# Reordering the layer-norm prologue and splitting the last output tiles of a linear-attention block

## The chip, the core and the metric

The kernel runs on one core of a Trainium2 chip. The metric is the device time of one execution in microseconds (us). The span in a profile is 1.4 to 1.8 us shorter than this time, and the difference will matter below. All times inside a profile count from the start of its span. PE is the matrix engine (PEld its weight loads), DVE is VectorE, ACT ScalarE, POOL GpSimd, SP SyncE.

## The reference

Layer norm of x, then a linear-attention branch s (32 heads of 20) and a gate g from a two-layer ReLU block, with S = 2048, D = 640, Dff = 1728, all bf16:

```python
xn = _layernorm(x, axis=-1)
s = _A_ref(xn, A_wqkv, A_wo)        # phi(q), phi(k): linear attention, then @ wo
g = _silu(_B_ref(xn, B_w1, B_w2))   # relu(xn @ w1) @ w2
return x + s * g
```

## The kernel before

The program is a list of operations per engine. Each engine runs its own list in order, and a helper derives the semaphore waits from what each operation reads (`R`) and writes (`W`). The 2048 tokens are 16 tiles of 128. Two places are touched: the head, in which tiles 0 to 3 are loaded, normalised and transposed and their keys computed, and the tail, in which the last two tiles are multiplied by g, added to x and stored.

```python
    KS = 3                                   # wk is loaded as 3 + 2 row blocks
    x_load(0)
    x_load(1)
    w_load(wqk[:, 0:KS, D:2 * D], A_wqkv[0:P * KS, D:2 * D], ("wk", 0))
    x_load(2)
    w_load(wqk[:, KS:C, D:2 * D], A_wqkv[P * KS:D, D:2 * D], ("wk", 1))
    x_load(3)
    # ... (cut)
    warm(34)                                 # matmuls without use, to wake PE's clock
    # ... (cut)
    # LN_stat(t, a): sums of half a of tile t (DVE).  LN_aggr: mean, variance (DVE).
    # LN_root_pool: 1/sqrt(var + eps) (POOL).  LN_stats = both LN_stat, LN_aggr, LN_root_pool.
    # LN_norm: (x - mean) * rs (DVE).  transposes: 5 on PE.  xnT_copy: PSUM to SBUF (ACT).
    # K_mm(t, bank, ks): 2 matmuls of 320 columns for each row block k in ks.
    LN_norm(0, late_loads)
    transposes(0, 4)
    warm(11)
    xnT_copy(0, 4)
    LN_stat(1, 1)
    LN_aggr(1)
    LN_root_pool(1)
    LN_stats(2)
    LN_norm(1)
    K_mm(0, 0, range(0, KS))
    transposes(1, 5)
    xnT_copy(1, 5)
    K_mm(0, 0, range(KS, C))
    LN_norm(2)
    warm(3)
    transposes(2, 6)
    xnT_copy(2, 6)
    K_mm(1, 2)
    K_exp(0, 0)
    K_relu(0, 0)
    LN_stats(3)
    LN_norm(3)
    K_mm(2, 5, range(0, KS))
    transposes(3, 4)
    xnT_copy(3, 4)
    K_mm(2, 5, range(KS, C))
    warm(3)
    # ... (cut: keys of tile 3, then queries, hidden layer, G, kv, W; U = second layer of the gate)
    U(0, kv_all)
    U(1, w_all)
    for p in range(2, 8):                    # U runs its hook between its two halves
        ts = pairs[p - 2] if p < 7 else pairs[5] + pairs[6]
        U(p, s_hook(ts, 0 if p % 2 == 0 else 4))
    pr[0] = 2
    for t in pairs[7]:
        s_tile(t, last=True)                 # last: multiply, add and store by halves
```

## Time and profile before

| | |
|---|---|
| time, median of 3 (at prediction) | 226.27 us (226.17 to 226.44) |
| span of the profiled run | 224.6 us |
| PE busy | 97% of the span |
| first weight load of the query matmuls | 14.17 us |
| end of PE's last matmul | 221.04 us |
| end of the last add on VectorE | 222.29 us |

Lines of the page of the kernel before: span, busy time by engine, PE's busy tenths and the granted clock in 40 slices, and the chain that ended last by engine.

```profile
span 224.6 us, 3494 instructions
...
PE 218.1 (97%) x1450; PEld 135.2 (60%) x1460; DVE 102.5 (46%) x191; ACT 88.3 (39%) x146; POOL 43.8 (20%) x62
...
PE   7999999999999999999999999999999999999993
...
PEclk9999999999999999999999999999999999999999
...
PE 92%; DVE 2%; DMA 2%; issue 1%; ACT 1%; SPq 1%; POOL 0%; DVEq 0%
```

PE is less than 90% busy only in the first and in the last slice. A change that leaves the real matmuls alone can gain time only there.

The head, from the chain of waits of the kernel before (start, us, what):

```profile
2.20 4.26 DMA reg<-in_A_x_dram
...
6.48 0.90 DVE stats L383 x2
7.40 0.22 DVE mv L387
...
7.70 0.32 POOL rsv L391
...
8.09 0.59 POOL rsy L393
...
8.70 0.46 DVE reg L412
...
9.21 0.45 PE psT L422 x5
9.66 2.17 PE psT L439 x16
11.83 0.32 PE psT L422 x5
...
12.17 0.71 ACT reg L427
...
12.93 1.55 PE psT L439 x10
```

The head hangs on the landing of x tile 2 at 6.48 us. Its sums, root and norm (8.70) lead to its transposes (9.21). Then come 16 key matmuls, the transposes of tile 3, their copy, and tile 3's matmuls at 12.93; the query matmuls follow without a gap.

The tail, from the timeline (start, us, engine, line, operation, shapes, count):

```profile
218.16 2.88 PE L796 MATMUL psT<-reg,pqT 128*128 128x320 bf16 x20
218.36 0.70 ACT L764 ACTIVATE reg<-psT 128x640 bf16<-128x640 f32 x1 [8.26 <-PE psT L768]
219.16 0.49 DVE L810 TENSOR_TENSOR reg<-psT,reg 128x320 bf16<-128x320 f32 x1 [2.99 <-ACT reg L764]
219.69 0.33 DVE L813 TENSOR_TENSOR reg<-reg 128x320 bf16<-128x320 bf16 x1
...
221.45 0.48 DVE L810 TENSOR_TENSOR reg<-psT,reg 128x320 bf16<-128x320 f32 x1
221.97 0.32 DVE L813 TENSOR_TENSOR reg<-reg 128x320 bf16<-128x320 bf16 x1
```

The last 20 matmuls end at 221.04. VectorE waits for the last silu (L764, ScalarE) and then works off four multiplies and four adds; the last ends 1.26 us past PE's end.

### The profile page before, as it was taken

What the parts mean: (1) busy time and instruction counts of PE and PEld (TensorE: products, weight loads), DVE (VectorE), ACT (ScalarE), POOL (GpSimd) and SP (SyncE); (2) the same over time, 40 slices, a digit from 0 to 9 for tenths busy, and PEclk for the clock granted to TensorE, in tenths of its full rate; (3) what the DMA queues carried; (4) which work ended last, traced back from release to release, by engine and by line L of the source; (5) the groups of instructions that cost most, each with busy time, mean ns of one, the idle gap of its engine ahead of it and who ended that gap; (6) DMA issues with size and microseconds to landing.
All of it is one profiled execution on the core that took longest, in us unless ns stands there. A gap on an engine that the chain in (4) does not pass through costs nothing.

```text
span 224.6 us, 3494 instructions
## 1 busy us (share of the span) xinstructions
PE 218.1 (97%) x1450; PEld 135.2 (60%) x1460; DVE 102.5 (46%) x191; ACT 88.3 (39%) x146; POOL 43.8 (20%) x62
## 2 busy tenths in 40 slices
PE   7999999999999999999999999999999999999993
PEld 7654555455554555444477778667767767776772
DVE  4599931796639872967000044440404041331445
ACT  4587765657665666654521122241021102102110
POOL 2436842322541255700000013000000000000000
PEclk9999999999999999999999999999999999999999
DMA  6999620012501150000999999500001010101021
GB/s 185 362 395 257 149 74 0 0 31 58 32 1 29 29 56 5 0 0 3 210 217 300 346 386 325 176 0 3 34 25 61 0 60 3 58 0 61 27 90 58
DMA packets 24239, 23.07 MB, mean 103 GB/s; under 512 B 8992, under 2 KB 23584, under 8 KB 24224
## 3 DMA queue, kind: packets, MB, share of 16 engines
q1 hardware_dynamic: 24224, 22.86, 35.7%
q8 instruction: 11, 0.18, 0.4%
q14 instruction: 4, 0.03, 0.1%
HBM read 15.65 MB, written 5.24 MB: 93 GB/s over the span
## 4 chain that ended last, share of the span: by engine, by line
PE 92%; DVE 2%; DMA 2%; issue 1%; ACT 1%; SPq 1%; POOL 0%; DVEq 0%
PE psT L768 25%; PE psT L514 25%; PE psT L702 10%; PE psT L491 10%; PE psT L439 9%; PE psT L796 8%; DMA reg<-in_A_x_dram 2%; PE psT L729 2%; PE psT L746 1%; PE psT L527 1%; DVE reg L810 1%; PE psT L714 1%; PE psT L610 1%; DVE reg L813 0%; DVE stats L383 0%
## 5 line engine op out<-in xcount | busy, mean ns | idle before, releaser
L768 PE MATMUL psT<-reg,hT 128*128 128x320 bf16 x416 | 58.7, 299 | 0.3
L514 PE MATMUL psT<-reg 128*128 128x512 bf16 x252 | 56.8, 379 | 0.5 <-issue 0.2
L768 PEld LDWEIGHTS psT<-reg,hT 128*128 128x128 bf16 x416 | 40.3, 98 | 17.0 <-PE psT L746 1.6
L514 PEld LDWEIGHTS psT<-reg 128*128 128x128 bf16 x260 | 25.2, 98 | 29.2 <-ACT hT L518 0.4
L764 ACT ACTIVATE reg<-psT 128x640 bf16<-128x640 f32 x16 | 10.8, 702 | 68.8 <-PE psT L746 35.4
L518 ACT ACTIVATE hT<-psT 128x512 bf16<-128x512 f32 x52 | 30.9, 599 | 17.7 <-PE psT L514 17.4
L810 DVE TENSOR_TENSOR reg<-psT,reg 128x640 bf16<-128x640 f32 (+1 forms) x18 | 13.5, 749 | 49.0 <-PE psT L796 45.9
L451 POOL TENSOR_TENSOR zacc<-zacc,reg 128x640 f32<-128x640 f32 x16 | 22.6, 1412 | 21.5 <-DVE reg L470 21.3
L439 PE MATMUL psT<-reg 128*128 128x320 bf16 x160 | 24.5, 299 | 0.1
L796 PE MATMUL psT<-reg,pqT 128*128 128x320 bf16 x160 | 22.9, 299 | 0.0
L702 PE MATMUL psT<-reg 128*128 128x320 bf16 x160 | 21.9, 299 | 0.0
L491 PE MATMUL psT<-reg 128*128 128x512 bf16 x98 | 21.8, 379 | 0.1
L439 PEld LDWEIGHTS psT<-reg 128*128 128x128 bf16 x160 | 15.4, 98 | 8.0 <-ACT reg L427 0.3
L702 PEld LDWEIGHTS psT<-reg 128*128 128x128 bf16 x160 | 15.6, 98 | 6.4 <-issue 0.4
L796 PEld LDWEIGHTS psT<-reg,pqT 128*128 128x128 bf16 x160 | 15.7, 98 | 6.1
L695 DVE TENSOR_TENSOR pqT<-pqT,reg 128x2048 bf16<-128x2048 bf16 x5 | 5.9, 1219 | 26.8 <-DMA reg<-rden_by_feature 26.8
L491 PEld LDWEIGHTS psT<-reg 128*128 128x128 bf16 x100 | 9.8, 98 | 11.2
L383 DVE BATCH_NORM_STATS2 stats<-reg 128x6 f32<-128x320 bf16 x32 | 14.1, 479 | 3.7 <-DMA reg<-in_A_x_dram 3.7
L498 ACT ACTIVATE er<-psT 128x512 bf16<-128x512 f32 x20 | 12.4, 619 | 8.6 <-PE psT L491 3.5
L456 ACT ACTIVATE ek<-psT 128x640 bf16<-128x640 f32 x16 | 11.3, 707 | 9.1 <-PE psT L439 9.1
L468 DVE TENSOR_SCALAR ek<-ek 128x640 bf16<-128x640 bf16 x16 | 5.5, 347 | 18.3 <-ACT ek L456 18.3
L508 DVE SCALAR_TENSOR_TENSOR pqT<-er 128x512 bf16<-128x512 bf16 x15 | 12.9, 859 | 0.5
(58 smaller groups left out, 139.2 us busy)
## 6 DMA issues: line engine op xcount, KB each, us to landing
reg<-in_A_x_dram SPq DMA_DIRECT2D x16, 160.0 KB, 5.3
rden_by_feature<-rden SPq DMA_DIRECT2D x4, 640.0 KB, 8.8
reg<-rden_by_feature SPq DMA_DIRECT2D x5, 512.0 KB, 11.1
reg<-in_A_x_dram SPq DMA_DIRECT2D x4, 640.0 KB, 6.8
reg<-in_B_w_dram SPq DMA_DIRECT2D x2, 1120.0 KB, 10.2
out_dram<-reg SPq DMA_DIRECT2D x14, 160.0 KB, 1.8
reg<-in_B_w_dram SPq DMA_DIRECT2D x1, 1040.0 KB, 10.2
reg<-in_B_w_dram SPq DMA_DIRECT2D x1, 960.0 KB, 14.8
```

Of the source, the lines that this page charges most:

```text
L383: sc.op("DVE", lambda eng: eng.bn_stats(stats[:, t, a, :], xin[:, t % XR, HN * a:HN * (a + 1)]), R=[("xin", t % XR)], W=[("stats", t, a)])
L439: fns.append(lambda eng, a=a, k=k: eng.matmul(ps[b + a][:, 0:HN], lhsT=xnT[:, k, tok(t)], rhs=wqk[:, k, D + HN * a:D + HN * (a + 1)], star ...
L451: sc.op("POOL", lambda eng: eng.tensor_tensor(out=zacc[:, :], in0=zacc[:, :], in1=pk[:, t, :], op=ALU.add), R=[("zacc",), ("pk", t)], W=[( ...
L491: sc.group("PE", [(lambda eng, k=k: eng.matmul(ps[b], lhsT=wqk[:, k, P * f:P * (f + 1)], rhs=xnT[:, k, schunk(j)], start=(k == 0), stop=(k ...
L498: sc.op("ACT", lambda eng: eng.activation(out=e_, in_=ps[b], func=ACTF.Exp), R=[("ps", b)], W=[("er_e", es)])
L508: sc.op("DVE", lambda eng: eng.scalar_tensor_tensor(out=pqT[:, f, schunk(j)], in0=e_, scalar=1.0, in1=r_, op0=ALU.min, op1=ALU.add), R=[(" ...
L514: a = sc.group("PE", [(lambda eng, k=k: eng.matmul(ps[b], lhsT=w1_sb[:, k, P * f:P * (f + 1)], rhs=xnT[:, k, schunk(j)], start=(k == 0), s ...
L518: sc.op("ACT", lambda eng: eng.activation(out=hT[:, f, schunk(j)], in_=ps[b], func=ACTF.Relu), R=[("ps", b)], W=[("hT", j, f)])
L702: fns.append(lambda eng, t=t, a=a: eng.matmul(ps[b + a][:, 0:HN], lhsT=xn[:, t, P * k:P * (k + 1)], rhs=pk[:, t, HN * a:HN * (a + 1)], sta ...
L768: fns = [(lambda eng, u=u, t=t, f=f, n=n: eng.matmul(ps[bs[n] + u][:, 0:HN], lhsT=hT[:, f, tok(t)], rhs=w2_sb[:, f, HN * n:HN * (n + 1)], ...
L796: sc.group("PE", [(lambda eng, c=c, a=a: eng.matmul(ps[b + a][:, 0:HN], lhsT=pqT[:, c, tok(t)], rhs=wf[:, c, HN * a:HN * (a + 1)], start=( ...
L810: sc.op("DVE", lambda eng: eng.tensor_tensor(out=tmpo[:, os_, lo:hi].rearrange(shp, a=na), in0=src, in1=g_sb[:, t, lo:hi].rearrange(shp, a ...
```

## The change

In the head, norm 1 is to run as soon as its root is there, between the two half sums of tile 2; tile 3 is loaded ahead of the rest of wk and its sums run ahead of norm 2; PE gets eight matmuls of tile 1 before the transposes of tile 2. In the tail, the left halves of the last two tiles move ahead of the last half of U; of the two right halves, one is added on GpSimd and stored from ScalarE's queue. The diff, cut to its core:

```diff
     x_load(2)
+    x_load(3)
     w_load(wqk[:, KS:C, D:2 * D], A_wqkv[P * KS:D, D:2 * D], ("wk", 1))
-    x_load(3)
-    warm(34)
+    warm(33)
# ... (cut)
-    LN_stats(2)
+    LN_stat(2, 0)
     LN_norm(1)
     K_mm(0, 0, range(0, KS))
     transposes(1, 5)
     xnT_copy(1, 5)
+    LN_stat(2, 1)
+    LN_aggr(2)
+    LN_root_pool(2)
+    warm(2)
     K_mm(0, 0, range(KS, C))
-    LN_norm(2)
-    warm(3)
-    transposes(2, 6)
-    xnT_copy(2, 6)
-    K_mm(1, 2)
     K_exp(0, 0)
     K_relu(0, 0)
     LN_stats(3)
+    LN_norm(2)
+    K_mm(1, 2, range(0, 4))
+    transposes(2, 6)
+    xnT_copy(2, 6)
+    K_mm(1, 2, range(4, C))
     LN_norm(3)
-    K_mm(2, 5, range(0, KS))
+    warm(3)
     transposes(3, 4)
     xnT_copy(3, 4)
-    K_mm(2, 5, range(KS, C))
-    warm(3)
+    K_mm(2, 5)
# ... (cut: s_half(t, a, bank, slot, addE, dmaE): 5 matmuls, multiply, add and store of half a of tile t)
-    for p in range(2, 8):
-        ts = pairs[p - 2] if p < 7 else pairs[5] + pairs[6]
-        U(p, s_hook(ts, 0 if p % 2 == 0 else 4))
-    pr[0] = 2
-    for t in pairs[7]:
-        s_tile(t, last=True)
+    for p in range(2, 7):
+        U(p, s_hook(pairs[p - 2], 0 if p % 2 == 0 else 4))
+    ea, eb = pairs[7]
+    oe = [(so[0] + 4) % NOUT, (so[0] + 5) % NOUT]
+    def last_hook():
+        s_hook(pairs[5] + pairs[6], 4)()
+        s_half(ea, 0, 0, oe[0])
+        s_half(eb, 0, 1, oe[1])
+    U(7, last_hook)
+    s_half(ea, 1, 4, oe[0], "POOL", "ACT")
+    s_half(eb, 1, 5, oe[1])
```

More of the change, by code (lines that the diff above doesn't have):

```diff
@@ L441, in K_mm @@
                     start=(k == 0), stop=(k == C - 1)))
-        wks = [0, 1] if ks is None else [0 if ks[0] < KS else 1]
+        wks = [0, 1] if ks is None else sorted({0 if k < KS else 1 for k in ks})
         sc.group("PE", fns, R=[("xnT", t)] + [("wk", i) for i in wks], W=[("ps", b), ("ps", b + 1)])
@@ L788, in bass_recurrent_scan__linear_attn_block__dense_activation_relu__prompt_kernel, with s_half, s_tile @@
     so = [0]
-    def s_tile(t, last=False):
+    def s_half(t, a, b, os_, addE="DVE", dmaE="SP"):
+        lo, hi = HN * a, HN * (a + 1)
+        sc.group("PE", [(lambda eng, c=c: eng.matmul(
+            ps[b][:, 0:HN], lhsT=pqT[:, c, tok(t)], rhs=wf[:, c, lo:hi], start=(c == 0), stop=(c == C - 1)))
+            for c in range(C)], R=[("pqT", t // 4, c) for c in range(C)] + [("wf", c, a) for c in range(C)], W=[("ps", b)])
+        sc.op("DVE", lambda eng: eng.tensor_tensor(out=tmpo[:, os_, lo:hi], in0=ps[b][:, 0:HN], in1=g_sb[:, t, lo:hi],
+                                                   op=ALU.mult), R=[("ps", b), ("g", t, a)], W=[("tmpo", os_, lo)])
+        sc.op(addE, lambda eng: eng.tensor_tensor(out=outb[:, os_, lo:hi], in0=tmpo[:, os_, lo:hi], in1=xre[:, t, lo:hi],
+                                                  op=ALU.add), R=[("tmpo", os_, lo), ("xre", t // 4)], W=[("outb", os_, lo)])
+        dma(dmaE, lambda eng: eng.dma_start(out2[tok(t), lo:hi], outb[:, os_, lo:hi]), R=[("outb", os_, lo)])
+    def s_tile(t):
         b = nextp()
@@ L816, in piece @@
             dma("SP", lambda eng: eng.dma_start(out2[tok(t), lo:hi], outb[:, os_, lo:hi]), R=kk("outb"))
-        if last:
-            piece(0, HN, b)
-            piece(HN, D, b + 1)
-        else:
-            piece(0, D, None)
+        piece(0, D, None)
     gb = [0, 2]
```

## The prediction

> **What bounds the kernel now.** The matrix engine: the busy table gives PE 97% of the 224.6 us span, the chain of waits 92%. The timeline shows PE without a gap worth naming from 12.93 us (matmuls of key tile 3) to 218.3 us, at full granted clock. Only the head before and the tail after can give time back. The change edits exactly these; all real matmuls stay, one warm-up matmul (0.11 us) fewer is issued.
>
> **Head.** In the chain, x tile 2 lands at 6.48 us, then its sums, aggregate (7.40), GpSimd root (7.70 to 8.67), norm 2 (8.70). Norm 1 stands behind the sums of tile 2 and starts at 7.53, although its root was ready at 6.78. Norm 3 runs at 11.18 and its transposed copy ends at 12.87; the matmuls of tile 3 wait for that (0.26 us idle, after 0.2 us of warm-up filler).
> After, from these durations: one half of the sums at 6.48, norm 1 at 6.95, its transposes at 7.55 (PE is free only then) instead of 7.98. Landings in the trace go 0.43 us apart per 160 KB, so x3 lands at about 7.0 instead of 7.77 and the wk rest at 7.8 instead of 7.35; it is used at about 7.95, so this hides. Norm 2 falls back to 9.1 (from 8.70), harmless since eight matmuls of tile 1 run ahead of its transposes. Norm 3 comes at about 10.1, 1.0 us earlier. Then transposes 2 at 9.9, their copy ready at 11.1, tile 2's matmuls from 11.15, tile 3's from 12.5 instead of 12.93. Gain 0.4 us, not the 1.0 us of norm 3: PE work and the copy of tile 2 are the next limit. It should carry through: wq lands at 11.3, PE reaches it at 14.3 now.
>
> **Tail.** Now the last 20 matmuls end at 221.0, but VectorE waits for the last silu (219.07) and then runs four multiplies (0.49 each) and four adds (0.33) to 222.29; the last store lands 1.6 us after issue. After, the two left halves are multiplied during the last matmuls of the g stage; only two multiplies and one add stay. Silu ends at about 220.4, the multiplies run at 220.5 and 221.1, the last add would end at 221.95. The other add goes to GpSimd, 221.1 to 221.8 (estimate: half of its 1.41 us for 640 columns). It collides: the Trainium skill, "GPSIMD Engine Reference", Specifications, states contention with VectorE instructions with two SBUF inputs; this trace agrees (a VectorE add of 0.43 us took 1.58 beside a GpSimd add). So the last VectorE add should wait and end at about 222.1. Gain 0.2 us, 0.35 without the collision. The second queue saves only issue time (0.33 us): the skill, "DMA: Bandwidth & Descriptors", Issuing engines are not separate DMA queues; no run shows it yet.
>
> **Sum.** 226.27 - 0.4 - 0.2 = 225.65 us; 8 in 10 between 225.1 and 226.2. Faster by over 2%: 1%; within 2%: 98%; slower: 1%.
>
> **What would show it.** Timeline: transposes 1 at 7.5, norm 3 near 10.1, tile 3's matmuls near 12.5, every later stage shifted by the same 0.4 us; the last multiply near PE's end; the last VectorE add longer than 0.33 us.
>
> **What would make it wrong.** The wk rest landing after 8 us; exp 0 and relu 0 delaying copy 2; the head's shift lost in a later wait; the first store on the ScalarE queue landing slower than 1.6 us, or the GpSimd add over 1 us, making the tail a small loss.

## The result and the profile after

| | before | after |
|---|---|---|
| time, median of 5 | 226.27 us (226.14 to 226.59) | 225.72 us (225.59 to 226.12) |
| ratio | | 0.9976 (95%: 0.9962 to 0.9991) |
| span of the profiled run | 224.6 us | 224.2 us |

Ratios here and below are the mean time of one kernel's fast runs over that of the other's of the same rounds, so they are not quite the ratio of the medians. The prediction was 225.65 us with a range of 225.1 to 226.2. The total agrees. The profile does not agree with the parts. The page of the changed kernel:

```profile
span 224.2 us, 3489 instructions
...
PE 218.3 (97%) x1448; PEld 135.4 (60%) x1458; DVE 102.5 (46%) x190; ACT 88.4 (39%) x146; POOL 44.6 (20%) x63
...
PE   7999999999999999999999999999999999999994
...
PE 95%; DVE 1%; DMA 1%; issue 1%; ACT 0%
```

The head of the changed kernel, lines of the timeline: the first half sum of tile 2, norm 1, the weight load of tile 1's transposes, norm 3, the matmuls of tiles 2 and 3, and the first query weight load:

```profile
7.03 0.49 DVE L383 BATCH_NORM_STATS2 stats<-reg 128x6 f32<-128x320 bf16 x1 [1.09 <-DMA reg<-in_A_x_dram]
...
7.44 0.43 DVE L412 TENSOR_SCALAR reg<-reg,mv,rsy 128x640 bf16<-128x640 bf16 x1
...
7.92 0.28 PEld L422 LDWEIGHTS psT<-ident,reg 128*128 128x128 bf16 x5 [0.18 <-DVE reg L412]
...
10.69 0.45 DVE L412 TENSOR_SCALAR reg<-reg,mv,rsy 128x640 bf16<-128x640 bf16 x1 [0.72 <-POOL rsy L393]
...
11.51 2.89 PE L439 MATMUL psT<-reg 128*128 128x320 bf16 x20
...
14.11 1.96 PEld L491 LDWEIGHTS psT<-reg 128*128 128x128 bf16 x10
```

Tile 2 landed at 7.03 instead of 6.48 us. The query start moved from 14.17 to 14.11: 0.06 us were gained in this pair of profiles, not 0.4.

The tail of the changed kernel, timeline:

```profile
219.45 1.52 PE L795 MATMUL psT<-reg,pqT 128*128 128x320 bf16 x10
219.65 0.70 ACT L767 ACTIVATE reg<-psT 128x640 bf16<-128x640 f32 x1 [9.62 <-PE psT L771]
220.46 1.04 DVE L798 TENSOR_TENSOR reg<-psT,reg 128x320 bf16<-128x320 f32 x2 [2.82 <-ACT reg L767]
221.03 0.79 POOL L800 TENSOR_TENSOR reg<-reg 128x320 bf16<-128x320 bf16 x1 [84.13 <-DVE reg L798]
221.53 0.47 DVE L800 TENSOR_TENSOR reg<-reg 128x320 bf16<-128x320 bf16 x1
221.85 0.37 ACTq L802 DMA_DIRECT2D out_dram<-reg  x1
```

PE ends at 220.97 and VectorE at 222.00, 1.03 us later instead of 1.26. The last add takes 0.47 us, as foreseen, beside the GpSimd add of 0.79.

So theory 1 was the prediction (head 0.4, tail 0.2), with the late landing of tile 2 a chance of this run. Its rivals: the new order of loads delays tile 2 and the head gives nothing, the whole gain being in the tail.

### The profile page after: what moved, and what is told of

The parts are those of the page before. It is cut to its first block, busy times and chain, and to the rows that moved or that the text cites. A ratio compares the mean times of both kernels' runs of the same rounds, so it can differ in the third digit from the quotient of the medians.

```text
span 224.2 us, 3489 instructions
## 1 busy us (share of the span) xinstructions
PE 218.3 (97%) x1448; PEld 135.4 (60%) x1458; DVE 102.5 (46%) x190; ACT 88.4 (39%) x146; POOL 44.6 (20%) x63
## 4 chain that ended last, share of the span: by engine, by line
PE 95%; DVE 1%; DMA 1%; issue 1%; ACT 0%
PE psT L771 26%; PE psT L514 25%; PE psT L705 10%; PE psT L491 10%; PE psT L439 10%; PE psT L810 8%; PE psT L732 2%; PE psT L795 1%; PE psT L749 1%; DMA reg<-in_A_x_dram 1%; PE psT L527 1%; PE psT L422 1%; PE psT L717 1%; PE psT L367 1%; DVE stats L383 1%; PE psT L613 1%
## 5 line engine op out<-in xcount | busy, mean ns | idle before, releaser
L824 DVE TENSOR_TENSOR reg<-psT,reg 128x640 bf16<-128x640 f32 x14 | 11.6, 825 | 46.0 <-PE psT L810 45.9
L810 PE MATMUL psT<-reg,pqT 128*128 128x320 bf16 x140 | 20.0, 299 | 0.0
L800 POOL TENSOR_TENSOR reg<-reg 128x320 bf16<-128x320 bf16 x1 | 0.8, 786 | 84.1 <-DVE reg L798 84.1
L810 PEld LDWEIGHTS psT<-reg,pqT 128*128 128x128 bf16 x140 | 13.7, 98 | 5.3
L383 DVE BATCH_NORM_STATS2 stats<-reg 128x6 f32<-128x320 bf16 x32 | 14.2, 479 | 4.2 <-DMA reg<-in_A_x_dram 4.2
## 6 DMA issues: line engine op xcount, KB each, us to landing
reg<-in_B_w_dram SPq DMA_DIRECT2D x1, 1040.0 KB, 10.1
```

What stands on the lines that cost most here:

```text
L383: sc.op("DVE", lambda eng: eng.bn_stats(stats[:, t, a, :], xin[:, t % XR, HN * a:HN * (a + 1)]), R=[("xin", t % XR)], W=[("stats", t, a)])
L810: sc.group("PE", [(lambda eng, c=c, a=a: eng.matmul(ps[b + a][:, 0:HN], lhsT=pqT[:, c, tok(t)], rhs=wf[:, c, HN * a:HN * (a + 1)], start=( ...
L824: sc.op("DVE", lambda eng: eng.tensor_tensor(out=tmpo[:, os_, lo:hi].rearrange(shp, a=na), in0=src, in1=g_sb[:, t, lo:hi].rearrange(shp, a ...
```

## The experiments

Four numbers are read from every profile: the landing of x tile 2 (where its first sum waits for it, that sum's start), the start of the first query weight load (the query start below), the end of PE's last matmul, and the end of the span. One fact makes this worthwhile: from the query start to PE's end it was 206.87 or 206.88 us in all 14 profiles. Anything gained or lost is in the head or in the tail. A head can therefore also be worked out for every timed run, as its span less the tail (PE's end to span's end of that kernel) less 206.87.

### The kernel before again, and the changed kernel again

No edit in either.

> The kernel before, unchanged, against itself: shows what repetition alone does. Both theories: ratio 1.000 within 0.15%, tile 3's matmuls from about 12.9 us, VectorE ends about 1.25 us after PE. The theory that x tile 2's landing varies from run to run (late landing in the one profile of the changed kernel is chance) expects its landing to differ from 6.48 us here by some tenths; the theory that the new order of loads makes it late expects 6.5 again.

> The changed kernel again. If the late landing of x tile 2 (7.03 us) was chance: it lands earlier here, tile 3's matmuls start near 12.5 instead of 13.0, span about 0.3 us under the first profile's 224.2. If the new load order causes it: 7.0 again. Either way ratio near 0.9976.

Before again: 226.5 us (226.03 to 226.91), ratio 1.0002 (0.9981 to 1.0023). Tile 2 landed at 7.20 and the query start fell to 14.89. Again from the chain of waits:

```profile
2.19 4.99 DMA reg<-in_A_x_dram
...
7.20 0.90 DVE stats L383 x2
...
13.65 1.53 PE psT L439 x10
```

Changed again: 226.03 us (225.52 to 226.22), ratio 0.9981 (0.9964 to 0.9998). Tile 2 landed at 6.33, but the query start was 14.13. So the landing of tile 2 is chance: the same transfer, issued at 2.2 us, lands anywhere between 6.3 and 7.2. That the new load order makes it late is refuted: over all profiles in which it is issued at 2.2 us it landed between 6.32 and 7.20 with the old order (four) and between 6.33 and 7.10 with the new one (six). But my expectation that an early landing would give a query start near 13.7 (tile 3's matmuls near 12.5) was missed too: something else held it.

### The head alone and the tail alone

Edits: the hunks above, up to `K_mm(2, 5)` in one kernel, from `s_half` on in the other.

> Change of the head alone, old tail. My theory (head gains 0.4 us, tail 0.2): 0.4 us faster, ratio about 0.998, start of the first query matmuls 0.4 us earlier than before if x tile 2 lands at 6.5; VectorE still ends 1.25 us after PE. Rival (the gain is nearly all in the tail, as in the first profile, where the head gained 0.1 us): ratio above 0.9995.

> Change of the tail alone, old head. My theory: 0.2 us faster, ratio about 0.999, VectorE ends 1.0 us after PE instead of 1.25, last add 0.47 us. Rival: 0.4 to 0.5 us faster, ratio about 0.998.

| | time, us | ratio (95%) | tile 2 lands | query start | DVE end after PE | span end after PE |
|---|---|---|---|---|---|---|
| head alone | 226.1 | 0.9986 (0.9969 to 1.0002) | 6.85 | 14.22 | 1.26 | 3.59 |
| tail alone | 226.53 | 1.0000 (0.9978 to 1.0022) | 6.32 | 14.03 | 1.03 | 3.19 |

The timing intervals include both theories' values; the rival's 0.998 for the tail lies just inside the edge of its interval. The profiles say more. In the three profiles with the old head and the old loads, query start minus landing is 7.69, 7.69 and 7.71 us. In the first two the chain of waits passes through the landing. In the third, the tail alone, it does not: with tile 2 at 6.32 us, tile 1's transposes waited for PE and not for their norm (norm 1 had ended at 7.76, their first weight load came at 7.98). So this difference is a coincidence, and the old head has a floor of its own. In the new head the three query starts (14.11, 14.13, 14.22) do not follow the landings (7.03, 6.33, 6.85).

### The order of computation without the load swap, and tile 2 late on purpose

The first keeps the new order of computation and puts the wk rest ahead of x3 again. The other two load tile 2 behind all of wk, with either order of computation (old tail in all three):

```diff
     w_load(wqk[:, 0:KS, D:2 * D], A_wqkv[0:P * KS, D:2 * D], ("wk", 0))
-    x_load(2)
     w_load(wqk[:, KS:C, D:2 * D], A_wqkv[P * KS:D, D:2 * D], ("wk", 1))
+    x_load(2)
     x_load(3)
```

> New order of the head's computation, loads in the old order (wk rest ahead of x3), old tail. Theory now: the load swap does nothing for the time, the computation order removes the dependence on x tile 2's landing, so the first query weight load starts at 14.1 to 14.2 us as long as x tile 2 lands before about 7.0, as with the swap. Rival: the swap matters, x3 (landing 7.8 to 8.5) holds the sums of tile 3, and the query start falls to 14.5 or later.

> Kernel before with x tile 2 loaded behind all of wk, so that it lands later on purpose (near 7.3 to 8.0 us). Theory: in the old order the query start follows the landing one for one, landing + 7.7 us (14.17-6.48, 14.89-7.20, 14.03-6.32 in three profiles), so 15.0 to 15.7. Rival (the old head is bound by PE work and the landing was a coincidence): near 14.2 to 14.9 again.

> New order of the head, old tail, x tile 2 loaded behind all of wk. Theory: the new order is insensitive only up to a landing of about 7.0; later than that norm 1 waits behind the one half of tile 2's sums, and the query start is landing + 7.1 us, that is 0.6 us earlier than the old order for the same landing: 14.4 to 15.1. Rival (new order insensitive altogether): 14.1 to 14.2.

| | time, us | ratio (95%) | tile 2 lands | query start | difference |
|---|---|---|---|---|---|
| new order, old loads | 225.79 | 0.9976 (0.9954 to 0.9998) | 6.67 | 13.75 | 7.08 |
| old order, tile 2 late | 227.23 | 1.0036 (1.0014 to 1.0058) | 8.18 | 15.86 | 7.68 |
| new order, tile 2 late | 226.79 | 1.0009 (0.9986 to 1.0033) | 8.07 | 15.15 | 7.08 |

Where the landing binds, the old head follows it with 7.7 us (landings of 6.48, 7.20 and 8.18). The new head follows with 7.08 when the tile is late: 0.6 us less. Both late starts lie just past the ranges that I expected (15.0 to 15.7 and 14.4 to 15.1), because the tile landed later than the 8.0 us that I had allowed; the sums held. The chain of waits of the last one shows why it still waits at all:

```profile
8.07 0.49 DVE stats L383
8.56 0.36 DVE reg L412
...
8.97 0.47 PE psT L422 x5
...
9.46 0.71 ACT reg L427
...
10.22 1.26 PE psT L439 x8
```

Norm 1 (L412) stands behind one half sum of tile 2 on VectorE, so tile 1's transposes at 8.97 wait for the landing of tile 2, of which they need nothing. That it is 7.08 and not 7.7 was confirmed by a later run of the new head in which tile 2 happened to land at 7.10 (the one-queue kernel below): query start 14.18. The first row and the changed kernel's own first profile (7.03 and 14.11) are the same sum. Their chains of waits do not name the landing, because PE's modelled ends overlap there, but the weight load of tile 1's transposes waited for norm 1 in both (0.19 us in the first row; 0.18 us in the line at 7.92 above), and norm 1 had run right behind tile 2's half sum.

The swap of loads is not needed for the gain: without it the query start was 13.75, the earliest of all new heads. My expectation there was 14.1 to 14.2 and its rival's 14.5 or later; it was better than both. It is one draw: by spans, the six runs of that kernel average 13.99 and those of the head with the swap 14.14, too close for these runs to separate.

### The warm-up

When tile 2 is early, what sets the new head? The starts of single matmuls show it. PE begins with 128-column matmuls every 106 ns and 320-column ones every 267 ns, and falls to 56 and 135 ns at some moment. That moment, in the new head with early tile 2: 5.55 us (query start 13.75), 5.99 (13.80), 7.43 (14.13), 7.65 (14.22). The first of these was held by the landing, so its floor is 13.75 or earlier. In the second the chain of waits runs through ScalarE's copy of tile 0 behind its table load (4.58 to 5.86), so that there it is not the warm-up that binds. The page and the windows show a granted clock of 1.00 throughout, but only because the trace has no clock record before this moment: in the raw trace the record of full clock begins at 5.50, 5.96, 7.30 and 7.56 us in these four. The test takes the first warm-up matmuls out of the changed kernel:

```diff
-    warm(33)
```

> Changed kernel without the 33 warm-up matmuls before the first transposes. In twelve profiles PE fell to its short matmul spacing 3.1 to 6.1 us after its first matmul, a different time each run, and the query start of the new head order seemed to depend on it when x tile 2 is early (13.75 and 13.80 with the fall at 5.5 and 6.0 us, 14.13 to 14.22 with 7.2 to 7.7). Theory: late warm-up costs, so with the first matmul at 5.3 us the fall comes at 8.4 to 11.4 us, the key matmuls run at the long spacing (0.27 instead of 0.135 us each) until then, and the query start falls to 14.5 to 16 us; time 0.5 to 1.5 us over the changed kernel. Rival (the warm-up does not bind, the spread has another source): query start at 13.7 to 14.2 again unless x tile 2 lands after 7.0.

Measured: 227.07 us (226.84 to 227.47), ratio to the kernel before 1.0027 (0.9998 to 1.0055). Tile 2 landed at 6.59, but PE fell to the short spacing only at about 9.8 us, 4.5 us after its first matmul, and the query start was 15.10. PE, timeline of this run:

```profile
5.36 0.72 PE L421 MATMUL psT<-ident,reg 128*128 128x128 bf16 x5 [5.36 <-DVE reg L411]
5.86 1.38 PE L367 MATMUL psT<-ident 128*128 128x128 bf16 x11
7.04 1.81 PE L438 MATMUL psT<-reg 128*128 128x320 bf16 x6
8.64 0.74 PE L421 MATMUL psT<-ident,reg 128*128 128x128 bf16 x5
```

Six key matmuls take 1.81 us here (0.99 in the first profile of the kernel before), and tile 1's transposes wait for PE rather than for their norm. So a late end of the warm-up does hold the query start; the rival falls. How far it explains the 13.80 to 14.22 of the other runs rests on the three profiles above alone. The time is about 1.2 us over the changed kernel's, as expected, if medians of different rounds are compared. The Trainium skill, "TensorE: Matmul & The Clock Gate", Part 1, says that the array starts at half clock and is released by a busy window of about 3.4 us that runs free of the kernel's start. The spacings agree (106 and 56 ns), and so does the chance in it: in the 14 profiles the fall came 3.1 to 6.1 us after the first matmul, a spread of 3.0 us, though the earliest is under 3.4. The raw clock records agree too: each shows full clock for 215.04, 218.45 or 221.87 us, which is 63, 64 or 65 windows of the page's 3413 ns.

### Tile 2 loaded first

Old order of computation and old tail, `x_load(2)` ahead of the first part of wk.

> Kernel before, old order of computation, old tail, only x tile 2 loaded ahead of the first part of wk. Theory (x tile 2's landing is what binds the old head): it lands near 4.1, the wait is gone, and the query start moves to 13.3 to 13.8, before that of the changed kernel (14.1), until PE work binds; 0.5 to 0.9 us faster than before, ratio about 0.997, and a smaller spread. Rival (the compute order matters, not the landing; or the first part of wk, now 0.4 us later, holds the first key matmuls): 14.1 or later.

Measured: 226.02 us (225.49 to 226.36), ratio 0.9977 (0.9958 to 0.9996), query start 14.30. Within the intervals this is the gain of the changed kernel, by one moved line. But the start of 13.3 to 13.8 was missed in the profile, in the way that the rival named: the first part of wk now landed at 7.44 and PE idled for it 1.25 us. The time was as expected only at the small end.

### The tail: one queue, and no GpSimd

Both on the changed kernel:

```diff
-    s_half(ea, 1, 4, oe[0], "POOL", "ACT")
+    s_half(ea, 1, 4, oe[0], "POOL", "SP")      # tail_one_queue
+    s_half(ea, 1, 4, oe[0], "DVE", "ACT")      # tail_dve_add
```

> Changed kernel, but the one store that ScalarE issues goes back to the SyncE queue (GpSimd add kept). So far every run with the new tail has 3.19 us from PE's last matmul to the end of the span (old tail 3.60) but 1.71 us between span and time (old tail 1.46), so only 0.15 of the 0.41 us is real. If the second queue causes that exchange: here both return, span minus PE's end to about 3.5 or more, time minus span to 1.46. If the rest of the new tail causes it: 3.2 to 3.4 and 1.71. The last store waits behind the one of the GpSimd add and lands about 0.15 us later than in the changed kernel.

> Changed kernel, but the third add runs on VectorE instead of GpSimd (second queue kept). Theory: the GpSimd add lengthens the last VectorE add from 0.33 to 0.47 us[...], so here the last add takes 0.33 us again, but it starts later behind the third: VectorE ends 1.10 us after PE instead of 1.03, and the last store lands in 1.63 us instead of 1.74 because the two last stores are further apart; in sum the same within 0.1 us. Rival (GpSimd takes real work off the end): 0.3 us later.

| tail | DVE end after PE | last store issued to landed | span end after PE | time minus span (mean) | last two added |
|---|---|---|---|---|---|
| before | 1.26 | 1.58 | 3.60 | 1.46 | 5.06 |
| changed | 1.03 | 1.69 | 3.19 | 1.71 | 4.90 |
| changed, one queue | 1.03 | 1.68 | 3.65 | 1.44 | 5.09 |
| changed, add on VectorE | 1.10 | 1.58 | 3.16 | 1.76 | 4.92 |

With one queue both the long end and the short difference are back. So the second queue itself moves 0.25 to 0.3 us from inside the span to outside of it: in the raw trace SyncE's last event comes 0.31 us after the other engines' last ones (224.62 against 224.30 in the kernel before), and beside them when ScalarE issues a store (224.10 and 224.11 in the changed kernel). Why, these runs do not show. What counts is the sum in the last column: the tail gains 0.16 us, not the 0.41 that the spans suggest. Timing alone does not separate this from zero.

The second queue is nonetheless needed. On one queue the very last store is issued behind the store of the GpSimd half, at 222.30 us instead of 222.03 (PE ended 0.08 later), and the gain is gone. The GpSimd add is not needed: with that add on VectorE the last add takes 0.33 us instead of 0.47, and the sum is the same within 0.02 us. So the collision is shown. The Trainium skill, "GPSIMD Engine Reference", Specifications, has it: GpSimd shares its SBUF interfaces with VectorE, and instructions with two SBUF inputs contend. The timeline of that run:

```profile
220.15 0.49 DVE L798 TENSOR_TENSOR reg<-psT,reg 128x320 bf16<-128x320 f32 x1 [2.82 <-ACT reg L767]
220.68 0.33 DVE L800 TENSOR_TENSOR reg<-reg 128x320 bf16<-128x320 bf16 x1
220.92 0.48 DVE L798 TENSOR_TENSOR reg<-psT,reg 128x320 bf16<-128x320 f32 x1
221.03 0.37 ACTq L802 DMA_DIRECT2D out_dram<-reg  x1
221.44 0.33 DVE L800 TENSOR_TENSOR reg<-reg 128x320 bf16<-128x320 bf16 x1
```

The times were 226.06 us, ratio 0.9967 (0.9947 to 0.9987), with one queue and 225.81 us, ratio 0.9961 (0.9944 to 0.9979), with the add on VectorE. These intervals are too wide to tell the two from each other or from the changed kernel.

### A version from these findings

```diff
-    KS = 3
+    KS = 2
     x_load(1)
+    x_load(2)
     w_load(wqk[:, 0:KS, D:2 * D], A_wqkv[0:P * KS, D:2 * D], ("wk", 0))
-    x_load(2)
# old order of computation, except:
-    K_mm(2, 5, range(0, KS))
+    K_mm(2, 5, range(0, 2))
# ... (cut)
-    K_mm(2, 5, range(KS, C))
-    warm(3)
+    K_mm(2, 5, range(2, C))
+    warm(1)
# tail: left halves as in the changed kernel; the last half of U tile by tile, silu after each,
# s_half(ea, 1, 4, oe[0]) between the two,
# all on VectorE and the SyncE queue; s of (eb, 1) as two groups of 160 columns,
# two multiplies, one add, one store
```

> A version meant to beat both: x tile 2 loaded ahead of wk, and the first part of wk cut from three to two of its five row blocks so that it lands no later (bytes ahead of it unchanged); old order of computation with tile 3's transposes after four of tile 2's matmuls; in the tail the last g pair is finished token tile by token tile, so that silu, multiply and add of the first are done before PE ends, and the very last half is multiplied in two quarters. Expected: x tile 2 lands at 4.1 to 5.2, query start at 13.3 to 13.7 (changed kernel 14.1), VectorE ends 0.7 us after PE (1.03), one queue so time minus span 1.46. About 225.2 us, 1.2 under before, 0.6 under the changed kernel; ratio 0.9945. If PE work binds the head regardless: query start stays at 14.0 and only 0.3 us of the tail is gained, ratio 0.9965.

Measured: 225.0 us (224.98 to 225.61), ratio 0.9933 (0.9918 to 0.9948), correct. The interval lies below the changed kernel's in the rounds that each was measured in (0.9962 to 0.9991), so it beats both. Its tail sums to 3.14 + 1.46 = 4.60 us, 0.30 less than the changed kernel's, although VectorE ends 0.80 us after PE and not 0.7. Its head, worked out from the spans of six timed runs (mean 223.70 less 3.14 less 206.87), has the query start at 13.69 us on average, against 14.02 for the eight runs of the two tail kernels, which have the changed head and ran in the same rounds. The profiled run, the slowest of the six, shows what binds now; chain of waits:

```profile
2.67 5.70 DMA reg<-in_A_wqkv_dram
...
8.50 0.97 PE psT L439 x6
```

The wk rest landed at 8.4 us in that run and held the key matmuls of tile 0. The landing has only changed places; the query start there was 14.13, outside the 13.3 to 13.7 expected for the profile, and tile 2 landed at 5.25, just past the 4.1 to 5.2 expected.

## Why the prediction was right or wrong

**What bounds the kernel: right.** The stretch between query start and PE's end was 206.87 us before and after; only head and tail moved.

**Head, "Gain 0.4 us": near on average, and not a constant.** The two kernels are best compared in the same rounds. By spans, the query start is on average 14.50 us in the 17 runs of the kernel before in the rounds of the two repeats (224.96 - 3.59 - 206.87) and 14.17 us in the 6 runs of the changed one (224.23 - 3.19 - 206.87): 0.33 us, with a standard error of about 0.15. (Over 46 runs of the kernel before, from all rounds and several chips, it is 14.61.) The step that failed is "x tile 2 lands at 6.48 us", taken as a property of the kernel. It landed between 6.3 and 7.2 by chance. The old head costs the later of landing + 7.7 and a floor, 14.03 in the one profile that shows it; the new head the later of landing + 7.08 and a floor. That floor was 13.80 to 14.22 in three profiles, later when PE's warm-up ended later. In the profiles the query start (tile 2's load issued at 2.2 us) ran from 14.03 to 14.89 with the old head and from 13.75 to 14.22 with the new one. So one pair of runs can show anything from a small loss to over 1 us, and that 0.4 came near the average is in part luck of the one profile from which it was read. The first pair of profiles has tile 2 late on the new side (7.03 + 7.08 = 14.11 against 6.48 + 7.69 = 14.17), and so shows 0.06.

**The times of the single steps: right only with an early warm-up and an early tile 2.** I read all PE durations from a profile in which the warm-up ended at 6.34 us. The run with the new order and old loads, where it ended at 5.55, has tile 1's transposes at 7.57 (predicted 7.55) and the matmuls of tiles 2 and 3 from 11.15 (predicted 11.15). But what held the transposes there was norm 1 behind the half sum of tile 2 (landing 6.67), not PE as the prediction had it. In the changed kernel's own profile they stand at 7.93 and 11.51, and norm 3 at 10.69 (predicted 10.1).

**"x3 lands at about 7.0 ... the wk rest at 7.8 ... so this hides": right, but idle.** It did hide, and the swap brought nothing that these runs can tell from what the order alone brought. In the changed kernel's own profile the wk rest landed at 8.23 us, past the 8 us that the prediction named as a danger, and tile 0's last four matmuls began right behind it, at 8.37. It cost nothing, because tile 1's matmuls waited for their copy until 9.18 anyway.

**Tail, "Gain 0.2 us": nearly right, 0.16.** VectorE's end was predicted at 222.1 and came at 222.00 (1.03 after PE). The collision on the last add was predicted and measured (0.33 to 0.47 us). Not foreseen was that the last store lands 1.69 us after its issue instead of 1.58, which takes back half of the 0.23 us. It went with how close the last two stores were issued: 1.68 and 1.69 with 0.38 and 0.18 us between them, 1.58 twice with 0.76; no run varies the distance alone. "The second queue saves only issue time (0.33 us)" was true in its words and undervalued: without the second queue the last store is issued 0.19 us later after PE's end and the sum is 0.19 us longer, which is more than the whole gain of the tail. It agrees with the Trainium skill, "DMA: Bandwidth & Descriptors", Issuing engines are not separate DMA queues.

**Sum.** 0.33 + 0.16 is 0.49 us by parts; the two timed comparisons gave ratios of 0.9976 and 0.9981, about 0.5 us. The head was worked out from the spans of the second of them, so this agreement with it is no independent proof. Head alone and tail alone fit too, but neither is separated from zero by timing.

What stays open: why a store from ScalarE shifts 0.25 us out of the span, and why a landing varies by 0.9 us.

## What to carry to other kernels

A time read from one profile of the first ten microseconds is one draw: repeat the profile of the unchanged kernel before costing a change there, and write each start as the later of several sums, not as one number. Do not put an operation that is ready behind one that waits for a load in the same engine's list. When a change touches the end of the kernel, compare the time and not only the span.

## What the Trainium skill lacked or had wrong

- "TensorE: Matmul & The Clock Gate", Part 1, puts the end of the warm-up at about 4 us of activity, 500 ns either way. In 14 profiles it came 3.1 to 6.1 us after the first matmul. The free-running window that the page gives as the reason fits the width of the spread; the stated tolerance does not. Between profiles of the new head that no landing held, the query start differed by up to 0.42 us (13.80 and 14.22).
- "DMA: Bandwidth & Descriptors" does not say how much the landing of one queued load varies from run to run. The same 160 KB load, fourth in its queue and issued at 2.2 us, landed between 6.3 and 7.2 us. The first of its 16 engines was done at 5.6 and 5.5 us in two profiles of the same kernel, the last at 6.5 in one and 7.2 in the other.
- The same page, Issuing engines are not separate DMA queues, calls the saved issue time usually small beside the transfer. It was small here too (0.19 us beside 1.69), but at the end of a kernel it was the difference between a gain of 0.16 us and none; the page does not say so.
- No page says that a store from ScalarE's queue changes what lies inside the span: time minus span was 1.44 to 1.47 us with one queue and 1.71 to 1.76 with two.
